# Where two sets of casts stand in ScalarE's order, and where three small tiles live, in a gated linear-attention kernel

## The chip, the cores and the metric

One core of one Trainium2 chip runs the whole kernel. The metric is device time in microseconds (us) for one launch; the time of a version is the median of its runs. TensorE (PE) does the matmuls, VectorE (DVE) and ScalarE (ACT) read and write its results in PSUM, GpSimd (POOL) works on SBUF alone, SyncE (SP) issues most of the transfers. Each engine runs its own instructions strictly in the order written for it: an instruction that waits holds up everything behind it on its engine.

## The reference, cut to what matters

```
xn  = layernorm(x)                                   # x: 2048 x 576
q, k, v = split(xn @ wqkv)                           # 32 heads of 18
phi(t) = concat(softmax(t @ w_phi), softmax(-(t @ w_phi)))   # per head
o   = phi(q) (phi(k)^T v) / (phi(q) . sum(phi(k)) + 1e-6)    # linear attention
s   = o @ wo
g   = silu((silu(xn @ w_gate) * (xn @ w_up)) @ w_down)       # F = 4608
out = x + s * g
```

All is fp32. A product of two fp32 operands is done as three matmuls of rounded parts: `split(hi, lo, src)` (line 57) makes `hi` by a cast on ACT (line 58) and `lo = src - hi` by a subtraction on DVE (line 59).

## The kernel before, in words

The kernel has four stages on the one core: layernorm, transposes and weight folding; the k/v stage, which sums phi(k)^T v over 16 row tiles; the q stage (lines 522 to 642); and the feed-forward part (FFN, from line 644), which takes two thirds of the time and is fed by gate/up weights (`gate_up_weights`, line 669), cast on ACT and subtracted on DVE, four pieces for each slice of the hidden layer.

**The q stage.** A query tile t has 128 rows; pairs of tiles go through a loop of nine steps (line 624). `q_tile` (line 558) makes the logits in the PSUM tile `p2` (line 563, 28 matmuls), then `softmax_parts` (line 273) takes the maximum and the minimum per head (line 278), subtracts them into the two halves of `e` (line 279) and takes two exponentials on ACT (line 282). After them VectorE has a chain of one tile: the sum `sm` (line 285), `ez = e * zb` (line 567), its sum `y` (line 569), five short ones, and the scaling of `e` (line 577). There is one `p2`: the next tile's logits wait until line 279 has read the present ones twice. `numer` (line 580) transposes `e` and multiplies with the k/v sums; `project` (line 598) multiplies with wo, which has been split into `WOH` and `WOL` by `split_wo` (line 533), copies each half row tile from PSUM into `so` on ACT (line 619) and stores it to `s_dram` from ACT's queue. In the last step of the loop (`last`) four such outputs remain: two share one `p2`, the third takes `p`, the fourth takes `p2` again. wo comes in by five loads into three staging tiles that borrow places of tiles used later: `oh`, `ol` and `ez` (lines 528 to 531).

**Filler for TensorE.** `early_tile` (line 113) does five of the 36 hidden slices early, so that TensorE has work while a chain runs on the others. Its products fill a bank `pe` with 14 matmuls; there are two banks. The first bank of a pair comes free by a silu on ACT (line 119), the second by a product on DVE (line 122). Its weights are split by lines 62 to 64. `tails` (line 541) prepares a part of the FFN's weights through the tile `tl` (two places): load, four subtractions on POOL, a cast on ACT (line 550), a subtraction on DVE (line 551), stores from POOL's queue.

**What sets the order.** The order on each engine is fixed when the program is built. The builder takes the order of the code as priority (`high_priority` lifts a block) and puts next the instruction of highest priority that it expects to be ready; what it expects to be ready early can thus come ahead of code written before it. `tc.issue_after(x)` queues the block's instructions **on x's engine** behind x; the block's instructions on other engines are not bound by it. A tile of a pool takes one of its tag's `bufs` places and holds it until its last reader has finished.

`read` collects the subtractions of line 279, which run on DVE; `split_wo` puts its instructions behind the last of the second query tile's.

Of the kernel before, what the change touches and what calls it, by code (L numbers as in the profile page):

```python
# [9 lines left out]
F32 = mybir.dt.float32  # L10
F32R = mybir.dt.float32r
AF = mybir.ActivationFunctionType
# [4 lines left out]
S, D, H, DH, F = 2048, 576, 32, 18, 4608  # L17
P = 128
# [5 lines left out]
HALF = D // 2  # L24
# [13 lines left out]
def heads(ap):  # L38
    return ap.rearrange("p (h d) -> p h d", d=DH)
# [7 lines left out]
def gated_hedgehog_kernel(ctx: ExitStack, tc, x, w_qk, w_v, w_phi, wo, w_gu, w_tail, w_down, ident_in, mask_in, out):  # L47
# [5 lines left out]
    nc = tc.nc  # L53
# [3 lines left out]
    def split(hi, lo, src):  # L57
        nc.scalar.copy(hi, src)  # L58
        nc.vector.tensor_sub(lo, src, hi)  # L59
# [53 lines left out]
    def early_tile(f, i, parts, js=(0, 1), banks=None):  # L113
        for j in js:
            pg, pu = banks or [eps.tile([P, BT], F32, name="pe") for _ in range(2)]
            xw(pg, i, j, slice(0, BT), *parts[0], False)
            h = epool.tile([P, BT], F32, name="h")
            with tc.high_priority():
                nc.scalar.activation(h, pg, AF.Silu)  # L119
            last = xw(pu, i, j, slice(0, BT), *parts[1], False)  # L120
            with tc.high_priority():
                nc.vector.tensor_mul(h, pu, h)
            nc.sync.dma_start(h_dram[i, f, :, j * BT:(j + 1) * BT], h)
        return last

    with ExitStack() as att:
        const = att.enter_context(tc.tile_pool(name="const", bufs=1))
        ident = const.tile([P, P], F32, name="ident")
# [7 lines left out]
        with ExitStack() as wst:  # L136
# [129 lines left out]
            kk = kst.enter_context(tc.tile_pool(name="kk", bufs=2, side="right", reuse_waits="tile"))  # L266
# [6 lines left out]
            def softmax_parts(ps, e):  # L273
                m = kk_pool.tile([P, 2, H], F32, name="m", bufs=1)
                p4 = ps[:, :, 0:HALF].rearrange("p a (h d) -> p a h d", d=DH)
                for s, op in enumerate((ALU.max, ALU.min)):
                    m3 = m[:, s].rearrange("p (a h) -> p a h", a=2)
                    nc.vector.tensor_reduce(m3, p4, axis=AX.X, op=op)
                    read.append(nc.vector.tensor_sub(e[:, s * D:(s + 1) * D].rearrange("p (a h d) -> p a h d", a=2, d=DH),
                                                     p4, m3.unsqueeze(3).to_broadcast([P, 2, H // 2, DH])))  # L280
                for s in range(2):
                    nc.scalar.activation(e[:, s * D:(s + 1) * D], e[:, s * D:(s + 1) * D], AF.Exp,
                                         scale=1.0 if s == 0 else -1.0)
                sm = kk_pool.tile([P, 2 * H], F32, name="sm")
                nc.vector.reduce_sum(sm, heads(e), axis=AX.X)
                return sm

            kk_pool, read = kk, []

            def kv_step(n, phi, v):  # L290
                for i in range(2 * NG):
# [108 lines left out]
            def k_tile(t):  # L400
                i0, j0, cols = block(t)
                pk = kps.tile([P, 2, 512], F32, name="p2")
                for i in range(2):
                    w = slice(i * HALF, (i + 1) * HALF)
                    xw(pk[:, i, 0:HALF], i0, j0, cols, KVWH[:, :, :, w], KVWL[:, :, :, w], True)
                phi = kk.tile([P, 2 * D], F32, name="phi", bufs=2)
                sm = softmax_parts(pk, phi)
                nc.vector.reciprocal(sm, sm)
                nc.vector.tensor_mul(heads(phi), heads(phi), spread(sm, 2 * H))
                return phi  # L410
# [111 lines left out]
        with ExitStack() as qst:  # L522
            qw = qst.enter_context(tc.tile_pool(name="qw", bufs=1, reuse_waits="tile"))
            qk = qst.enter_context(tc.tile_pool(name="qk", bufs=2, reuse_waits="tile"))
# [1 line left out]
            WOH = qw.tile([GW, NG, D], F32R, name="WOH")  # L526
            WOL = qw.tile([GW, NG, D], F32R, name="WOL")
            wrs = [qk.tile([P, 2, D], F32, name="oh", bufs=1), qk.tile([P, 2, D], F32, name="ol", bufs=1),
                   qk.tile([P, 2, D], F32, name="ez", bufs=1)]
            for g, (o, w) in enumerate(GROUPS):  # L530
                nc.sync.dma_start(wrs[g // 2][0:w, g % 2], wo[o:o + w, :])

            def split_wo():
                with tc.issue_after(read[-1].ins):
                    for n, wr in enumerate(wrs):
                        g, w = slice(2 * n, min(2 * n + 2, NG)), GROUPS[2 * n][1]
                        split(WOH[0:w, g], WOL[0:w, g], wr[0:w, 0:min(2, NG - 2 * n)])

            kk_pool = qk
# [58 lines left out]
            def project(b, oh, ol, last):  # L598
                for j in range(QS // P):
                    pair = qps.tile([P, 2, 512], F32, name="p2") if last and j == 0 else None  # L600
                    jc = slice(j * P, (j + 1) * P)
                    r0 = b * QS + j * P
                    for i in range(2):
                        n = slice(i * HALF, (i + 1) * HALF)
                        if pair:
                            ps = pair[:, i]
                        elif last and i:
                            ps = qps.tile([P, 2, 512], F32, name="p2")[:, 0]
                        else:
                            ps = qps.tile([P, 512], F32, name="p")  # L610
                        k = 0
                        for g, (o, w) in enumerate(GROUPS):
                            for a, bw in ((oh, WOH), (oh, WOL), (ol, WOH)):
                                nc.tensor.matmul(ps[:, 0:HALF], a[0:w, g, jc], bw[0:w, g, n], start=k == 0,  # L614
                                                 stop=k == 3 * NG - 1)
                                k += 1
                        so = qk.tile([P, HALF], F32, name="so", bufs=2)
                        with tc.high_priority() if last else ExitStack():
                            nc.scalar.copy(so, ps[:, 0:HALF])
                        nc.scalar.dma_start(s_dram[r0:r0 + P, n], so)  # L620

            order = list(range(S // QS // 2, S // QS)) + list(range(S // QS // 2))
# [1 line left out]
            for n in range(S // QS + 1):  # L624
                new = []
                if n > 0:
                    om = numer(es)
                if n < S // QS:
                    new += [q_tile(order[n] * (QS // P) + j) for j in range(QS // P)]
                if n == 0:  # L630
                    split_wo()
                if n > 0:
                    project(order[n - 1], *om, n == S // QS)
                es = new
# [34 lines left out]
    def gate_up_weights(i, f):  # L669

        parts, wt = {}, fw.tile([96, 7, P], F32R, name="wt", bufs=2)
        n, q = divmod(f - EARLY, 4)
        if i == 0:
            ld = fw.tile([P, 2, D], F32, name="ld", bufs=2).rearrange("p a b -> p (a b)")
            ld = ld[:, 0:8 * P].rearrange("p (m c n) -> p m c n", m=4, c=2)
            nc.sync.dma_start(ld, w_gu[f, :, :, 0:2])
            ts = fw.tile([P, D], F32, name="ts")[:, 0:4 * P].rearrange("p (m c n) -> p m c n", m=2, c=2)

        def ready(m, src):
            k = 1 if m == 6 else 2  # L680
            w = fw.tile([P, k, 4, P], F32R, name=f"w{k}", bufs=2 if k == 1 else 4)
            if i:
                nc.sync.dma_start(w.bitcast(F32), w_dram[f - EARLY, :, m:m + k])
            else:
                split(w[:, :, 0:2], w[:, :, 2:4], src)
                if f < NF - 1:
                    nc.sync.dma_start(w_dram[f - EARLY, :, m:m + k], w.bitcast(F32))
            for c in range(k):
                parts[m + c] = w[:, c]

        ready(0, None if i else ld[:, 0:2])
        nc.sync.dma_start(wt.bitcast(F32), t_dram[n, q].rearrange("b r m n -> (b r) m n"))
        if i == 0:
            nc.gpsimd.tensor_sub(ts[:, 0], ld[:, 2], ld[:, 0])
            nc.gpsimd.tensor_sub(ts[:, 1], ld[:, 3], ts[:, 0])
            nc.gpsimd.tensor_sub(ld[:, 2], ld[:, 3], ld[:, 2])
            nc.gpsimd.tensor_sub(ld[:, 1], ld[:, 1], ts[:, 1])  # L697
        ready(4, None if i else ts)
        ready(2, None if i else ld[:, 2:4])
        ready(6, None if i else ld[:, 1:2])  # L700
        return parts, wt
# [319 lines left out]
    todo = [(i, f) for i, n, f in units if f >= EARLY and (i == 0 or f < NF - 1)]  # L1021
# [5 lines left out]
        nc.sync.dma_start(t, w_down[f * P:(f + 1) * P, :])  # L1027
    xo = operands(0)
    early_tile(EARLY - 1, 0, parts)
    ready = [gate_up_weights(*todo.pop(0))]  # L1030
    est.close()
    fq = ctx.enter_context(tc.tile_pool(name="fq", bufs=1, reuse_waits="tile"))
    fps = ctx.enter_context(tc.tile_pool(name="fps", bufs=1, space=PSUM, reuse_waits="tile"))
# [72 lines left out]
```

## Time and profile before

| | |
|---|---|
| median of 3 runs | 1637.58 us (1636.6 to 1639.58) |
| the profiled execution | 1638.38 us, of which its span 1636.6 us |
| busy in the span | PE 1604.0, DVE 1168.5, ACT 721.9, POOL 653.3 us |
| q stage, from its first logits | 229.7 us on |
| last output copy of the q stage | 483.92 us |
| first FFN product with gate/up weights | 512.6 us |

A row of the timeline gives the start, the length, the engine and line, the operation with the tile written and the tiles read, the count of merged instructions, and in brackets how long the engine stood idle before it and what ended that wait. A row of the windows gives, for one stretch of the span, its length and then the busy time of each engine in it with the count of instructions. Times are us from the span's start.

### The profile page before, as it was taken

How to read it: one execution, taken by the hardware profiler on the slowest of the kernel's cores; microseconds unless marked ns; L12 is line 12 of the kernel's file. 1: busy time of each engine (PE TensorE's matmuls, PEld its weight loads, DVE VectorE, ACT ScalarE, POOL GpSimd, SP SyncE). 2: the span in 40 equal slices, each digit the busy share in tenths (PEclk: the TensorE clock that was granted, in tenths of full speed). 3: DMA queues.
4: the chain of work that ended last, by engine and by line, in shares of the span. 5: the costliest groups of instructions: out<-in, count | busy, mean ns of one | idle time of the engine just before them, and what ended most of it. 6: DMA issues, size and time to landing. Idle time of an engine off the chain costs nothing.

```text
span 1636.6 us, 25198 instructions
## 1 busy us (share of the span) xinstructions
PE 1604.0 (98%) x9385; PEld 1429.7 (87%) x9385; DVE 1168.5 (71%) x1721; ACT 721.9 (44%) x1391; POOL 653.3 (40%) x699
## 2 busy tenths in 40 slices
PE   6999998999999999999999999999999999999998
PEld 5899997999978888888888888888888888888887
DVE  7677768899952678778777778825666766666578
ACT  5533345444432554544444544455433433333334
POOL 3485661333212455455545355313233324133132
PEclk9999999999999999999999999999999999999999
DMA  9622243334248545555554554684454655555444
GB/s 286 206 80 78 85 134 117 117 103 126 67 144 306 184 165 175 179 178 168 177 180 165 175 192 152 224 296 150 136 162 135 199 184 170 172 179 185 140 115 174
DMA packets 121741, 268.46 MB, mean 164 GB/s; under 512 B 12787, under 2 KB 53363, under 8 KB 119827
## 3 DMA queue, kind: packets, MB, share of 16 engines
q1 hardware_dynamic: 106652, 246.49, 45.9%
q0 software_dynamic: 3072, 11.02, 2.4%
q10 hardware_dynamic: 11894, 9.35, 1.8%
q8 instruction: 74, 1.21, 0.3%
q14 instruction: 49, 0.39, 0.1%
HBM read 167.19 MB, written 99.61 MB: 163 GB/s over the span
## 4 chain that ended last, share of the span: by engine, by line
PE 90%; DMA 4%; DVE 3%; POOL 1%; issue 1%; ACT 1%; SPq 0%; ACTq 0%; POOLq 0%; DVEq 0%
PE px L707 24%; PE pd L832 24%; PE pw L707 12%; PE py L707 6%; PE p L92 6%; PE pe L92 5%; PE p L614 4%; PE po L594 2%; PE kvp L294 2%; PE vx L382 1%; PE pt L588 1%; DMA xn<-in_A_x 1%; PE vw L382 1%; DMA s_dram<-so 1%; DMA sraw<-in_A_w_v 1%
## 5 line engine op out<-in xcount | busy, mean ns | idle before, releaser
L832 PEld LDWEIGHTS pd<-dw,hh 128*128 128x128 f32 x3048 | 432.4, 188 | 26.4 <-DVE dw L59 1.7
L832 PE MATMUL pd<-dw,hh 128*128 128x288 f32 x3048 | 448.5, 297 | 4.3 <-DVE dw L59 1.5
L707 PE MATMUL px<-X,w 128*128 128x512 f32 x1488 | 384.3, 393 | 0.0
L707 PEld LDWEIGHTS px<-X,w 128*128 128x128 f32 x1488 | 270.6, 188 | 51.8 <-ACT s L736 2.0
L707 PE MATMUL pw<-X,w 128*128 128x512 f32 x732 | 188.7, 393 | 0.0
L707 PEld LDWEIGHTS pw<-X,w 128*128 128x128 f32 x732 | 137.0, 188 | 30.5
L741 DVE TENSOR_TENSOR s<-pw,s 128x512 f32<-128x512 f32 x124 | 85.1, 688 | 100.0 <-ACT s L736 89.2
L957 DVE TENSOR_TENSOR acc<-pd,acc 128x576 f32<-128x576 f32 x128 | 96.2, 752 | 83.8 <-PE pd L832 83.6
L736 ACT COPY s<-px 128x512 f32<-128x512 f32 x124 | 72.6, 585 | 157.2 <-PE px L707 157.2
L92 PE MATMUL pe<-X,wh 128*128 128x512 f32 (+1 forms) x380 | 121.8, 401 | 5.8 <-ACT h L119 2.9
L59 DVE TENSOR_TENSOR hh<-ha,hh 128x512 fp32r<-128x512 f32 x140 | 111.5, 823 | 20.7 <-ACT hh L58 19.1
L58 ACT CAST hh<-ha 128x512 fp32r<-128x512 f32 x140 | 82.7, 619 | 92.4 <-PE pd L832 73.5
L929 POOL TENSOR_TENSOR hb<-hb 128x512 f32<-128x512 f32 x34 | 47.0, 1381 | 168.6 <-DVE hb L753 161.4
L59 DVE TENSOR_TENSOR w<-ld,w 128x512 fp32r<-128x512 f32 (+1 forms) x93 | 77.2, 832 | 35.7 <-ACT w L58 34.5
L707 PE MATMUL px<-X,wt 96*128 96x512 f32 x248 | 97.9, 395 | 0.0
L707 PE MATMUL py<-X,w 128*128 128x512 f32 x372 | 96.5, 394 | 0.0
L916 POOL TENSOR_TENSOR h<-ha,hb 128x512 f32<-128x512 f32 x34 | 44.3, 1302 | 126.8 <-DVE ha L757 88.6
L942 POOL TENSOR_TENSOR ha<-ha 128x512 f32<-128x512 f32 x34 | 52.6, 1564 | 103.5 <-DVE hh L59 103.5
L58 ACT CAST w<-ld 128x512 fp32r<-128x512 f32 (+1 forms) x93 | 51.0, 549 | 89.6 <-POOL ld L697 56.8
L92 PEld LDWEIGHTS pe<-X,wh 128*128 128x128 f32 (+1 forms) x380 | 70.0, 189 | 21.7 <-ACT h L119 3.4
L761 ACT COPY py<-px 128x512 f32<-128x512 f32 x62 | 35.5, 572 | 102.7 <-PE px L707 80.8
L707 PEld LDWEIGHTS py<-X,w 128*128 128x128 f32 x372 | 66.7, 188 | 11.2
(262 smaller groups left out, 3199.0 us busy)
## 6 DMA issues: line engine op xcount, KB each, us to landing
w_dram<-w SPq DMA_DIRECT2D x90, 512.0 KB, 2.9
w<-w_dram SPq DMA_DIRECT2D x90, 512.0 KB, 4.5
wt<-t_dram SPq DMA_DIRECT2D x61, 336.0 KB, 3.7
ld<-in_B_w_gu SPq DMA_DIRECT2D x31, 512.0 KB, 4.5
X<-sum_dram SPq DMA_DIRECT2D x8, 1280.0 KB, 11.1
rt<-in_B_w_down SPq DMA_DIRECT2D x33, 288.0 KB, 3.1
rb<-in_B_w_down SPq DMA_DIRECT2D x33, 288.0 KB, 4.7
w_dram<-w SPq DMA_DIRECT2D x30, 256.0 KB, 2.1
```

Of the source, the lines that this page charges most:

```text
L58: nc.scalar.copy(hi, src)
L59: nc.vector.tensor_sub(lo, src, hi)
L92: last = nc.tensor.matmul(ps, l, r, start=n == 0, stop=n == len(pairs) - 1)
L614: nc.tensor.matmul(ps[:, 0:HALF], a[0:w, g, jc], bw[0:w, g, n], start=k == 0, stop=k == 3 * NG - 1)
L707: nc.tensor.matmul(ps, l, r, start=first and n == 0, stop=last and n == len(mm) - 1, skip_group_check=True)
L736: nc.scalar.copy(t, ps)
L741: nc.vector.tensor_add(t, ps, t)
L832: nc.tensor.matmul(ps, l, r, start=first and n == 0 and m == 0, stop=n == len(hs) - 1 and m == 2, skip_group_check=True)
L916: sub(s, g["h"][0][0], g["h"][0][1])
L929: nc.gpsimd.tensor_add(a21, a21, g["h"][1][1])
L942: sub(a12, a12, g["h"][0][0])
L957: nc.vector.tensor_add(a2, pd[:, :, 0:HALF], a2)
```

## The change

Two edits, each with a change of place for the tiles it concerns.

- `split_wo`'s block is bound to `exps[-1]`, the second exponential of the second query tile on ACT, in place of `read[-1]` on DVE. The casts into `WOH` are now behind that exponential; the subtractions into `WOL` are bound only by needing the casts.
- The third staging tile of wo takes one of the four places of `e`, no longer the one place of `ez`.
- All output copies are collected in `outs`; the first call of `gate_up_weights` is queued on ACT behind the last of them.
- In the last step of the q loop, the second half row tile of each output goes through a place of `tl`, no longer of `so`.

```diff
+    outs = []
...
-                    nc.scalar.activation(e[:, s * D:(s + 1) * D], e[:, s * D:(s + 1) * D], AF.Exp,
-                                         scale=1.0 if s == 0 else -1.0)
+                    last = nc.scalar.activation(e[:, s * D:(s + 1) * D], e[:, s * D:(s + 1) * D], AF.Exp,
+                                                scale=1.0 if s == 0 else -1.0)
+                exps.append(last)
...
-            kk_pool, read = kk, []
+            kk_pool, read, exps = kk, [], []
...
             wrs = [qk.tile([P, 2, D], F32, name="oh", bufs=1), qk.tile([P, 2, D], F32, name="ol", bufs=1),
-                   qk.tile([P, 2, D], F32, name="ez", bufs=1)]
+                   qk.tile([P, 2 * D], F32, name="e", bufs=4).rearrange("p (a n) -> p a n", a=2)]
...
             def split_wo():
-                with tc.issue_after(read[-1].ins):
+                with tc.issue_after(exps[-1].ins):
...
-                        so = qk.tile([P, HALF], F32, name="so", bufs=2)
+                        if last and i:
+                            so = qk.tile([P, 7, P], F32, name="tl", bufs=2).rearrange("p a n -> p (a n)")[:, 0:HALF]
+                        else:
+                            so = qk.tile([P, HALF], F32, name="so", bufs=2)
                         with tc.high_priority() if last else ExitStack():
-                            nc.scalar.copy(so, ps[:, 0:HALF])
+                            outs.append(nc.scalar.copy(so, ps[:, 0:HALF]))
...
-    ready = [gate_up_weights(*todo.pop(0))]
+    with tc.issue_after(outs[-1].ins):
+        ready = [gate_up_weights(*todo.pop(0))]
```

## Prediction

> **What bounds the kernel now.** The page comes first: how much of the span is TensorE's own work.
>
> ```profile
> span 1636.6 us, 25198 instructions
> PE 1604.0 (98%) x9385; PEld 1429.7 (87%) x9385; DVE 1168.5 (71%) x1721; ACT 721.9 (44%) x1391; POOL 653.3 (40%) x699
> ```
>
> TensorE is idle for 1636.6 - 1604.0 = 32.6 us. The change removes no matmul, so it can win only idle time of TensorE, in the places that it reaches. The windows show how much lies there: length of the stretch, then PE, PEld, DVE, ACT and POOL busy.
>
> ```profile
> 240.00:280.00 40.00, 35.84 (x205) 30.68 (x205) 34.21 (x51) 22.00 (x28) 7.59 (x16) 1.00 0.46 146
> 280.00:460.00 180.00, 179.99 (x1235) 165.89 (x1234) 164.07 (x259) 80.68 (x144) 54.48 (x112) 1.00 0.33 100
> 470.00:490.00 20.00, 17.93 (x94) 14.25 (x93) 7.94 (x11) 7.04 (x15) 7.32 (x8) 1.00 0.72 238
> ```
>
> At the start of the q stage TensorE is idle for 40.00 - 35.84 = 4.16 us, at its end for 20.00 - 17.93 = 2.07 us, and between them for 0.01 us in 180. So 6.2 us, 0.38% of the time, is all that there is to win. TensorE's timeline shows it as six waits:
>
> ```profile
> 255.40 0.50 PE L92 MATMUL pe<-X,wh 128*128 128x512 f32 x1 [1.19 <-ACT h L119]
> 260.49 0.50 PE L92 MATMUL pe<-X,wh 128*128 128x512 f32 x1 [1.55 <-DVE h L122]
> 270.36 0.37 PE L92 MATMUL p<-QH,X 128*128 128x288 f32 x1 [1.42 <-DVE e L279]
> ...
> 477.94 0.40 PE L614 MATMUL p<-WOH,oh 126*128 126x288 f32 x1 [1.17 <-ACT so L619]
> 485.39 0.50 PE L92 MATMUL pe<-X,wh 128*128 128x512 f32 x1 [0.28 <-ACT h L119]
> 489.57 0.47 PE L92 MATMUL pe<-X,wh 128*128 128x512 f32 x1 [0.63 <-ACT h L119]
> ```
>
> I call them A, B, C and D, E1, E2. A and B wait for a filler bank that ACT or DVE frees late, C for the logits' only tile, which DVE reads late, D for an output copy. Why these engines are late is in their own timelines, ACT first:
>
> ```profile
> 239.61 1.26 ACT L282 ACTIVATE e<-e 128x576 f32<-128x576 f32 x2
> 244.86 1.16 ACT L58 CAST WOH<-oh 126x1152 fp32r<-126x1152 f32 x1 [3.99 <-DMA oh<-in_A_wo]
> 248.05 1.16 ACT L58 CAST WOH<-ol 126x1152 fp32r<-126x1152 f32 x1 [2.04 <-DMA ol<-in_A_wo]
> 249.12 0.66 ACT L58 CAST WOH<-ez 72x576 fp32r<-72x576 f32 x1
> 251.19 0.94 ACT L550 CAST th<-tl 128x896 fp32r<-128x896 f32 x1 [1.41 <-POOL tl L549]
> 252.04 0.68 ACT L282 ACTIVATE e<-e 128x576 f32<-128x576 f32 x1
> ...
> 254.75 0.60 ACT L119 ACTIVATE h<-pe 128x512 f32<-128x512 f32 x1
> ...
> 256.66 0.69 ACT L282 ACTIVATE e<-e 128x576 f32<-128x576 f32 x1
> ```
>
> After the first tile's exponentials ACT stands still for wo's transfers (3.99 and 2.04 us) and then for the tail's (1.41). The second tile's exponentials and the silu that ends A come behind all that. VectorE:
>
> ```profile
> 243.00 1.35 DVE L285 TENSOR_REDUCE sm<-e 128x64 f32<-128x1152 f32 x1
> ...
> 246.51 0.76 DVE L279 TENSOR_TENSOR e<-p,m 128x576 f32<-128x576 f32 x1
> 247.19 1.35 DVE L59 TENSOR_TENSOR WOL<-oh,WOH 126x1152 fp32r<-126x1152 f32 x1
> 253.47 0.69 DVE L63 TENSOR_TENSOR wl<-raw,wh 128x512 fp32r<-128x512 f32 x1 [4.94 <-ACT wh L62]
> ...
> 255.90 0.75 DVE L59 TENSOR_TENSOR WOL<-ez,WOH 72x576 fp32r<-72x576 f32 x1
> ...
> 257.24 1.34 DVE L567 TENSOR_TENSOR ez<-e,zb 128x1152 f32<-128x1152 f32 x1
> ...
> 259.76 0.68 DVE L122 TENSOR_TENSOR h<-pe,h 128x512 f32<-128x512 f32 x1
> ...
> 269.46 0.75 DVE L279 TENSOR_TENSOR e<-p,m 128x576 f32<-128x576 f32 x1
> ```
>
> It stands idle for 4.94 us up to 253.47 and then runs without a break. The first tile's `ez` product at 257.24 could have run at 244.35, when `sm` was done, but its place held the last wo rows until 255.90 + 0.75 = 256.65. So `ez` and what follows it come when they delay the product that ends B (259.76) and the subtraction that ends C (269.46).
>
> **The change part by part.**
>
> *The place of the last wo rows.* No instruction is added. `ez` of the first tile can start at 244.35 and fill the hole. What fits: `ez` (1.34, the row at 257.24), the sum `y` of the same size (I take 1.34), and the short ones, in all up to the 4.94 us that are idle now, less the 1.35 of `WOL<-oh`, which leaves its place at 247.19 for a later one. VectorE is thus ahead by up to 4.94 at 253 and has then 1.35 more to do: a net lead of 3.59 us. At most, that is: if only `ez` and `y` go forward, it is 2.68 - 1.35 = 1.33. B is 1.55 and C 1.42. The lead needn't pay both: TensorE, once B is gone, arrives at C 1.55 us earlier, so both together need 2.97. I take the larger end, 3.59, since the whole chain of the first tile is free to run in that hole and no other work of VectorE's is ready there. **B and C go: 2.97 us.** The price is that the second tile's subtractions of line 279 may come behind `ez` and `y`, later by up to 2.68 us than 246.51; the logits of the third tile wait for that, and filler covers it as long as a bank is free. The fourth place of `e` is first wanted by the fourth tile, whose logits start at 270.36, long after the rows have been split; I cost that at nothing.
>
> *The binding of the casts.* It takes 1.16 + 1.16 + 0.66 = 2.98 us of casts out of ACT's wait for wo and puts them behind the exponential that now ends at 256.66 + 0.69 = 257.35. That gains little at A: `th<-tl` at 251.19 comes later in the code than the second tile's exponentials, yet stands ahead of them in ACT's order, so the builder expects it to be ready sooner. It will still stand there, and still wait until 251.19. The silu that ends A comes behind it. From below A could shrink to nothing, if the silu comes ahead of that cast; from above it could grow by the 2.98 us of the casts, if these come ahead of the silu. I take **A as it is, 1.19**, since the row at 251.19 doesn't move. Behind the casts are queued the silus and exponentials after 257.35; ACT is busy for only 22.00 of the 40 us, and that hides 2.98. WOH and WOL are first read much later:
>
> ```profile
> 276.76 0.38 PE L614 MATMUL p<-WOH,oh 126*128 126x288 f32 x1
> ```
>
> The casts would end near 257.35 + 2.98 = 260.3, the subtractions (1.35, one like it, 0.75: 3.45 us) soon after, with some 12 us to spare.
>
> [...] VectorE would now run products of two SBUF tiles beside POOL's four subtractions for the tail, which end at 251.16 and release `th<-tl`. What that costs POOL can be read elsewhere in this trace:
>
> ```profile
> 477.12 0.72 POOL L694 TENSOR_TENSOR ts<-ld 128x256 f32<-128x256 f32 x1 [46.30 <-DMA ld<-in_B_w_gu]
> 483.69 1.07 POOL L694 TENSOR_TENSOR ts<-ld 128x256 f32<-128x256 f32 x1 [3.33 <-DVE w L59]
> 483.48 2.70 DVE L59 TENSOR_TENSOR w<-ld,w 128x512 fp32r<-128x512 f32 x3
> ```
>
> The same subtraction took 0.72 us alone and 1.07, half as much again, while VectorE subtracted from SBUF. The four subtractions before 251.16 lie in 1.95 us (1.41 of them as ACT's wait), so half as much again is about 1 us more, and `th`, the silu and A would all be later by that. It is a rival below. [...]
>
> *The end of the q stage.* ACT's order there:
>
> ```profile
> 473.36 0.40 ACT L619 COPY so<-p 128x288 f32<-128x288 f32 x1 [1.02 <-PE p L614]
> ...
> 476.97 0.62 ACT L58 CAST w<-ld 128x512 fp32r<-128x512 f32 x1 [3.22 <-DMA ld<-in_B_w_gu]
> 477.50 0.39 ACT L619 COPY so<-p 128x288 f32<-128x288 f32 x1
> 481.18 0.40 ACT L619 COPY so<-p 128x288 f32<-128x288 f32 x1 [3.29 <-DMA s_dram<-so]
> ```
>
> The second copy stands behind a weight cast that waits 3.22 us for its load; the fourth output's matmuls wait for that copy, and this is D. With the cast behind all four copies, the second runs at about 473.8, and **D goes: 1.17 us**. The third copy's 3.29 us wait for a place goes too, with four places for four outputs; `tl` is free, since POOL's last store from it is issued well before:
>
> ```profile
> 428.83 2.00 POOL L554 DMA_DIRECT2D t_dram<-tl  x4 [3.34 <-DVE tl L551]
> ```
>
> The added wait: the first weight's casts wait for the fourth copy, where the first started at 476.97. The fourth output's last matmul:
>
> ```profile
> 479.92 0.30 PE L614 MATMUL p<-WOH,ol 72*128 72x288 f32 x1
> ```
>
> Without D it ends at 480.22 - 1.17 = 479.05, so the casts start about 2.5 us later than now. Behind them on ACT are the casts of the second weight and the filler's silus. The weights are first wanted at 512.8:
>
> ```profile
> L707 PE MATMUL px<-X,w x1488: 387/393/501, 512.8 to 1612.5; 128*128 128x512 f32 x186
> ```
>
> More than 30 us of filler cover that. E1 and E2 (0.91 together) are silus that come late among these casts. They may go or stay, or double; I leave them.
>
> *The sum:* B 1.55 + C 1.42 + D 1.17 = 4.14 us. The profiled execution took 1638.38 (span 1636.6 and 1.78 around it), so 1634.24; it lies 0.80 above the median of the three runs, so **1633.4** as a median.
>
> **The rivals.** All are given as medians.
>
> *Nothing is left of the six waits.* The silu of A comes ahead of `th`, or the order gives TensorE the third tile's logits to do meanwhile, and E1 and E2 go with the lighter load. For: ACT has 10 us between 240.87 and 251.19 in which it now has nothing to do. Against: the silu must be ready by then in the builder's expectation, and it stood behind `th`. 6.23 us less: 1631.3.
>
> *The first edit does not do what it says.* The wait for wo was never the last one: ACT stands at `th` until 251.19 with or without wo's casts, the second tile's exponentials come when they came, the builder puts VectorE's chain where it was, and B and C remain. For: the 1.41 us wait at 251.19 is the one that ends last. Against: the `ez` place. Only D goes: 1636.4.
>
> *Slower: the casts get in front of a bank's release.* They used to lie inside a wait; now they are work in the busiest place. If the order puts the three between the second tile's exponential and the silu that ends A, A grows by 2.98. If VectorE's order does not use the hole, `WOL<-oh` leaves it, and VectorE, which has no idle time from 253.47 on, is later by 1.35 at B and again at C, since each of these waits is for its own instruction. It decides at the order: from the point at which that silu stands behind the casts. For: silu and exponential already alternate there. Against: the silu has `high_priority`, the casts have none. At most 2.98 + 1.35 + 1.35 - 1.17 = 4.5 us more: 1642.1.
>
> *POOL's share.* The forecast with `th` later by about 1 us: 1634.4.
>
> **How the numbers follow.** A measurement of this kernel tells about 0.2%, 3.3 us, from no change. Chances: forecast 0.45 (own range 1632.0 to 1635.0), no waits left 0.15, only D 0.23, slower 0.13, POOL's share 0.04. Faster by over 0.2% means under 1634.3: all of "no waits left" and nearly all of the forecast, 0.57. Slower by over 0.2% means above 1640.9; of the slower rival, whose price is an upper one, I count most, 0.12. The rest, 0.31, is within 0.2%. The range is 1631.0 to 1639.0: it holds all but the slower rival and a tail on either side.
>
> **What would show it.** In the profile of the changed kernel: the window 240 to 280 with TensorE busy about 38.8 us, and only the wait for `h L119` near 255 left; VectorE's `ez` of the first tile before 250 and no 4.94 us idle; ACT's first instruction after about 241 is not a cast of `WOH`, and `th` still starts near 251.2; four output copies in a row, none waiting for `s_dram`, and no TensorE wait for `so`. The prediction is wrong if `th` moves, if TensorE shows a new wait for `p2` or `pe` of over 2 us, or if stretches that the change does not name (280 to 460, or after 490) lose or win more than 1 us.

## The result, and the profile after

The changed kernel takes **1710.25 us** (median of 6 runs, 1707.43 to 1712.79) where the kernel before, beside it, takes 1638.77: a ratio of 1.0439 (95% interval 1.0427 to 1.0450), 71.5 us slower. The forecast was 1633.4. Both edits do what the diff says, and something that neither names costs ten times what they could win.

The page of the changed kernel first: span, busy times, and TensorE, POOL and the granted clock in 40 slices of 42.8 us.

```profile
span 1710.9 us, 25186 instructions
...
PE 1616.3 (94%) x9385; PEld 1438.1 (84%) x9385; DVE 1168.8 (68%) x1721; ACT 722.0 (42%) x1391; POOL 653.5 (38%) x699
...
PE   6999999999993299999999999999999999999998
...
POOL 3476640000045754644653544522342243132222
PEclk9999999999996599999999999999999999999999
```

TensorE's idle time is 1710.9 - 1616.3 = 94.6 us against 32.6, +62.0. Its busy time has grown as well, by 12.3 us, with the same 9385 matmuls; together that is the 74.3 us by which the span grew. Most of both lies in slices 13 and 14 of TensorE's row, and there the clock row falls to 6 and 5 tenths. POOL's row shows something else, and earlier: five slices of nothing, from the seventh on. The windows (length, then PE, PEld, DVE, ACT and POOL busy, clock, DMA share, GB/s) put numbers on that:

```profile
280.00:460.00 180.00, 179.90 (x1213) 164.41 (x1213) 151.85 (x245) 74.91 (x136) 0.00 (x0) 1.00 0.09 32
470.00:490.00 20.00, 20.00 (x124) 17.66 (x125) 8.07 (x14) 8.89 (x19) 3.62 (x5) 1.00 0.40 126
490.00:538.00 48.00, 37.77 (x147) 29.36 (x146) 8.73 (x12) 8.20 (x14) 22.67 (x43) 0.91 0.88 311
538.00:546.00 8.00, 0.00 (x0) 0.00 (x0) 1.09 (x1) 0.06 (x1) 7.36 (x16) 0.50 0.61 172
546.00:900.00 354.00, 305.81 (x1644) 267.94 (x1645) 245.13 (x342) 161.07 (x318) 199.19 (x234) 0.92 0.53 176
```

From 280 to 460 POOL did 54.48 us of work before; now it does none, and TensorE is still full. From 470 to 490 TensorE has no idle time any more: D, E1 and E2 are gone, as meant (a new wait of 0.79 us, for the filler's product, stands at 497). After 490 it stands for 10.2 + 8.0 + 48.2 us. What went missing is seen by tile: `tl`, in which the tails are prepared, first before and then after (instructions, shortest/median/longest in ns, first and last start in us).

```profile
L544 SPq DMA_DIRECT2D tl<-in_B_w_tail x8: 327/328/429, 243.0 to 401.6; - x8
L546 POOL TENSOR_TENSOR tl<-tl x8: 452/462/672, 249.2 to 410.4; 128x128 f32<-128x128 f32 x8
```

```profile
L546 SPq DMA_DIRECT2D tl<-in_B_w_tail x8: 328/332/533, 486.3 to 574.7; - x8
L548 POOL TENSOR_TENSOR tl<-tl x8: 465/466/910, 489.6 to 582.0; 128x128 f32<-128x128 f32 x8
...
L552 ACT CAST th<-tl x8: 935/937/942, 493.8 to 584.0; 128x896 fp32r<-128x896 f32 x8
...
L624 ACT COPY tl<-p x2: 400/400/401, 484.0 to 486.8; 128x288 f32<-128x288 f32 x2
```

All eight tails, loaded from 243 to 402 before, are now loaded from 486.3 on: the first of them takes the place that the first output copy (484.0) and its store leave. What this costs TensorE is in its timeline, all its waits from 500 to 640:

```profile
519.15 0.80 PE L712 MATMUL px<-X,wt 96*128 96x512 f32 x1 [3.38 <-DMA wt<-t_dram]
585.49 2.93 PE L712 MATMUL px<-X,w 128*128 128x512 f32 x6 [53.56 <-ACT s L741]
589.62 2.93 PE L712 MATMUL px<-X,w 128*128 128x512 f32 x6 [0.77 <-ACT s L741]
600.10 4.85 PE L712 MATMUL px<-X,w 128*128 128x512 f32 x12 [5.05 <-DVE hb L758]
609.37 1.65 PE L712 MATMUL px<-X,w 128*128 128x512 f32 x6 [0.46 <-ACT s L741]
616.97 1.32 PE L837 MATMUL pd<-dw,hh 128*128 128x288 f32 x8 [1.58 <-DVE dw L59]
625.17 1.66 PE L712 MATMUL px<-X,w 128*128 128x512 f32 x6 [0.74 <-ACT s L741]
```

First the FFN waits for a tail itself (`wt` is read from `t_dram`); then, for 53.56 us, for a plain copy from PSUM on ACT. That copy has no wait of its own. It stands behind casts that do, in ACT's timeline:

```profile
537.12 0.94 ACT L552 CAST th<-tl 128x896 fp32r<-128x896 f32 x1 [9.22 <-POOL tl L551]
546.35 0.94 ACT L552 CAST th<-tl 128x896 fp32r<-128x896 f32 x1 [8.29 <-POOL tl L551]
...
584.02 0.94 ACT L552 CAST th<-tl 128x896 fp32r<-128x896 f32 x1 [8.76 <-DMA t_dram<-tl]
584.86 0.58 ACT L741 COPY s<-px 128x512 f32<-128x512 f32 x1
```

Six tails in a row, 9.2 to 9.7 us apart. POOL sets this pace:

```profile
538.36 4.02 POOL L556 DMA_DIRECT2D t_dram<-th  x8 [0.59 <-ACT th L552]
542.36 2.00 POOL L556 DMA_DIRECT2D t_dram<-tl  x4
544.38 0.47 POOL L548 TENSOR_TENSOR tl<-tl 128x128 f32<-128x128 f32 x1
```

Twelve stores of 0.5 us each to issue, then four subtractions in the 1.97 us from 544.38 to the next cast at 546.35, that cast, 537.12 to 538.36 with its way to POOL: 6.02 + 1.97 + 1.24 = 9.23. This is the reading to take along from the view: the line that TensorE waits for (L741) is blameless, and one looks at what stands in front of it on its engine.

### The profile page after: what moved, and what is told of

The parts are those of the page before. It is cut to its first block, busy times and chain, and to the rows that moved or that the text cites. A ratio compares the mean times of both kernels' runs of the same rounds, so it can differ in the third digit from the quotient of the medians.

```text
span 1710.9 us, 25186 instructions
## 1 busy us (share of the span) xinstructions
PE 1616.3 (94%) x9385; PEld 1438.1 (84%) x9385; DVE 1168.8 (68%) x1721; ACT 722.0 (42%) x1391; POOL 653.5 (38%) x699
## 4 chain that ended last, share of the span: by engine, by line
PE 86%; DMA 4%; POOL 4%; DVE 3%; issue 1%; ACT 1%; ACTq 0%; SPq 0%; POOLq 0%; DVEq 0%
PE px L712 23%; PE pd L837 23%; PE pw L712 11%; PE p L92 6%; PE py L712 6%; PE pe L92 4%; PE p L616 4%; POOL t_dram L556 2%; PE po L596 2%; PE kvp L296 2%; PE vx L384 1%; DMA t_dram<-tl 1%; PE pt L590 1%; DMA xn<-in_A_x 1%; PE vw L384 1%
## 5 line engine op out<-in xcount | busy, mean ns | idle before, releaser
L712 PE MATMUL px<-X,w 128*128 128x512 f32 x1488 | 390.2, 398 | 60.6 <-ACT s L741 55.5
L699 POOL TENSOR_TENSOR ts<-ld 128x256 f32<-128x256 f32 x31 | 26.8, 865 | 329.3 <-DMA ld<-in_B_w_gu 254.7
L741 ACT COPY s<-px 128x512 f32<-128x512 f32 x124 | 72.7, 586 | 156.6 <-PE px L712 156.6
L59 DVE TENSOR_TENSOR w<-ld,w 128x512 fp32r<-128x512 f32 (+1 forms) x93 | 77.3, 832 | 36.2 <-ACT w L58 35.1
```

The source lines that it names most:

```text
L712: nc.tensor.matmul(ps, l, r, start=first and n == 0, stop=last and n == len(mm) - 1, skip_group_check=True)
L741: nc.scalar.copy(t, ps)
```

## The experiments

TensorE's idle time and its busy time are told apart, since both differ; each line is the profiled execution, with the clock granted from 240 to 280. The medians and ratios (95% intervals) are of all runs, against the kernel before on the same chip. Of the idle time 15.7 to 18.2 us lie ahead of 120 us, in stages that no edit touches, so a difference of one or two us in that column doesn't speak of an edit by itself; the single waits do.

| version | median us, ratio | span | PE busy | PE idle | clock 240 to 280 |
|---|---|---|---|---|---|
| before | | 1636.6 | 1604.0 | 32.6 | 1.00 |
| changed | 1710.25, 1.0439 | 1710.9 | 1616.3 | 94.6 | 0.96 |
| e2_tl_only | 1705.11, 1.0409 (1.0395 to 1.0423) | 1703.4 | 1615.2 | 88.2 | 0.91 |
| e8_no_lift | 1713.0, one run | 1711.1 | 1616.5 | 94.6 | 0.91 |
| e1_out_ph | 1643.48, 1.0033 (1.0020 to 1.0046) | 1643.9 | 1606.5 | 37.4 | 0.91 |
| e3_tails_first | 1643.38, 1.0031 (1.0020 to 1.0042) | 1639.5 | 1604.4 | 35.1 | 1.00 |
| e4_wo_only | 1641.32, 1.0014 (1.0003 to 1.0024) | 1639.9 | 1606.8 | 33.1 | 0.91 |
| e5_bind_only | 1640.10, 1.0020 (1.0009 to 1.0031) | 1639.8 | 1607.3 | 32.5 | 0.96 |
| e6_place_only | 1643.19, 1.0042 (1.0029 to 1.0056) | 1643.8 | 1608.5 | 35.3 | 0.91 |
| e9_both_bound | 1644.30, 1.0045 (1.0032 to 1.0058) | 1642.9 | 1607.1 | 35.8 | 0.91 |
| e11_late_e | 1644.19, 1.0034 (1.0021 to 1.0048) | 1642.5 | 1607.2 | 35.3 | 0.96 |
| e7_out_only | 1637.15, 0.9998 (0.9989 to 1.0007) | 1637.5 | 1605.5 | 32.0 | 1.00 |
| e12_ph_only | 1638.53, 1.0002 (0.9993 to 1.0011) | 1637.1 | 1603.6 | 33.5 | 1.00 |
| e10_bind_out | 1636.93, 0.9996 (0.9988 to 1.0005) | 1636.2 | 1603.4 | 32.8 | 1.00 |

**The theory** after the result: places of a tile are promised in the order of the code. The last `project` stands in the code ahead of the loop that writes the tails, so its two outputs take the two places of `tl` first, and every tail is put behind them. Rivals: the first edit upsets the tails (it moves the casts that `th` stood among); or the `high_priority` on the output copies pulls the tile forward.

### Where the tails went

*The one suspect line alone.* The kernel before, with only this:

```diff
-                        so = qk.tile([P, HALF], F32, name="so", bufs=2)
+                        if last and i:
+                            so = qk.tile([P, 7, P], F32, name="tl", bufs=2).rearrange("p a n -> p (a n)")[:, 0:HALF]
+                        else:
+                            so = qk.tile([P, HALF], F32, name="so", bufs=2)
```

> The kernel before with only the place of the last outputs' second halves changed, so to tl; no binding is added. Theory (places): this line alone brings the loss, 1700 to 1715, with POOL idle from 280 to 460 and a wait of some 50 us near 535. Rival (binding): the loss needs the weight casts bound behind the outputs; then this one is within 1630 to 1645.

Measured 1705.11, +66.7 us of the 71.5. By tile, the tails moved as in the changed kernel, and TensorE waits for the same copy:

```profile
L544 SPq DMA_DIRECT2D tl<-in_B_w_tail x8: 327/332/595, 484.7 to 566.3; - x8
```

```profile
576.98 2.93 PE L710 MATMUL px<-X,w 128*128 128x512 f32 x6 [45.59 <-ACT s L739]
```

*The whole change, the halves through another tile's place* (`ph`, whose last regular use is ahead of these outputs in the code):

```diff
-                            so = qk.tile([P, 7, P], F32, name="tl", bufs=2).rearrange("p a n -> p (a n)")[:, 0:HALF]
+                            so = qk.tile([P, 2 * QS], F32, name="ph", bufs=2)[:, 0:HALF]
```

> The changed kernel with one thing different: the second half of the last outputs goes through a place of ph, no longer of tl. Theory (places): the eight tails came after the q stage only because the outputs, written earlier in the code, hold the two places of tl; without that the tails are back between 250 and 430 us, POOL is busy there again, the 53.6 us wait of TensorE is gone, and what is left is the two small wins seen in the changed kernel's windows (TensorE idle 2.4 in place of 4.2 us in 240 to 280, 0 in place of 2.1 in 470 to 490): about 1635, 1632 to 1637. Rival (wo): the late casts of wo or the bound weight casts push the tails and the first weights back by themselves: 1700 or more as before, POOL still idle from 280 to 460.

Measured 1643.48: 66.8 us below the changed kernel by the medians. The tails' loads are back at 243.0 to 398.6. But the time is not the expected 1632 to 1637: about 5 us above the kernel before are left, and the next part looks for them.

*The whole change with `tl` kept, but the tails written first.*

```diff
+                if n == S // QS:
+                    for m in range(TAILS):
+                        with tc.issue_after(last_e[3 * m // 2 + 2].ins):
+                            tails(m)
                 if n > 0:
                     project(order[n - 1], *om, n == S // QS)
                 es = new
-            for n in range(TAILS):
-                with tc.issue_after(last_e[3 * n // 2 + 2].ins):
-                    tails(n)
```

> The changed kernel, tl for the outputs kept, but the loop that writes the tails stands in the code ahead of the last project. Theory (places are promised in the order of the code): the tails get the places first, the outputs after them: no loss, 1632 to 1638. Rival (the copies' high_priority takes the places, or tl is too small for both): still 1700 or more.

Measured 1643.38, again above the expected 1632 to 1638. The outputs still use `tl`; only the order of two blocks in the code has changed, and that is worth 66.9 us:

```profile
L546 SPq DMA_DIRECT2D tl<-in_B_w_tail x8: 327/328/430, 242.3 to 394.0; - x8
...
L624 ACT COPY tl<-p x2: 399/400/400, 485.1 to 487.8; 128x288 f32<-128x288 f32 x2
```

*The whole change, the copies not lifted.*

```diff
-                        with tc.high_priority() if last else ExitStack():
+                        with ExitStack():
```

> The whole change, but the last outputs' copies without high_priority, so that the code asks for the two places of tl in the same order and only the order on ACT can move. Theory (places of tl are given in the order of the code, the outputs standing ahead of the tails): as the change, about 1710 us, POOL without work from 241 to about 482. Rival (the lift of the copies pulls their places ahead of the tails): the tails return to 250 to 410, POOL works there, and the time is about 1640.

One run: 1713.0, and the tails as in the changed kernel:

```profile
L546 SPq DMA_DIRECT2D tl<-in_B_w_tail x8: 328/333/517, 486.0 to 574.9; - x8
```

So the cause of the large loss is settled: not the first edit, not the lift, but the order in which the code asks for the places of `tl`.

### The first edit

*Alone, both halves of it* (the kernel before with the binding to the exponentials and the rows in `e`):

> The kernel before with the first edit alone: casts of wo behind the second query tile's exponentials, last wo rows in a place of e. Theory (places): this part is a small win, TensorE idle in 240 to 280 down from 4.2 to about 2.4 us, so 1635 to 1638. Rival (wo): it costs, by casts and subtractions in the busy stretch from 255 on: 1641 or more, with new waits of TensorE for pe or p.

*Its binding alone* (`issue_after(exps[-1].ins)`, the last wo rows left in `ez`):

> The kernel before with the casts of wo bound behind the second query tile's exponentials, and nothing else; the last wo rows stay in ez. Theory (place): the new waits of TensorE at the start of the q stage (0.7 and 1.65 us near 242) come from the place in e, not from the binding: here VectorE's first subtractions into e stay near 234.5, right behind the maximum. ez of the first tile is late as before, so B and C stay in some form: 1637 to 1641. Rival (binding): the binding moves them, and they show here too.

*Its place alone* (rows in `e`, the binding left at `read[-1]`):

> The kernel before with the last wo rows in a place of e, and nothing else. Theory (place): the first query tile now gets another place of e, the builder holds it ready later, and the filler's product (line 122) goes ahead of the first subtraction into e: VectorE idle for some 5.8 us near 236 to 242, TensorE waiting 0.7 and 1.65 us near 242: about 1641, 1639 to 1644. Rival (binding): the first subtraction stays near 234.5, and the time is at or under that of before.

Measured 1641.32, 1640.10 and 1643.19: each slower than before, the place by 6.0 us. For the whole edit the rival came true and not the small win; the binding and the place came out within their ranges. The table splits what the profiled executions lose: the whole edit 2.8 us of busy time and 0.5 of idle, the binding 3.3 of busy time and none of idle, the place 4.5 and 2.7. So more than half is TensorE working longer at the same matmuls; that part is taken up in the last section, the waits here.

In TensorE's timeline of the version with everything but the lost tails (e3_tails_first), the first stretch of the q stage has these waits:

```profile
241.73 0.47 PE L92 MATMUL pe<-X,wh 128*128 128x512 f32 x1 [0.70 <-DVE h L122]
243.85 0.37 PE L92 MATMUL p<-QH,X 128*128 128x288 f32 x1 [1.65 <-DVE e L280]
254.43 0.50 PE L92 MATMUL pe<-X,wh 128*128 128x512 f32 x1 [0.52 <-ACT h L119]
256.25 0.37 PE L92 MATMUL p<-QH,X 128*128 128x288 f32 x1 [1.33 <-DVE e L280]
```

B and C are gone, as forecast, and A has shrunk to 0.52. But 0.70 + 1.65 at 242 and 1.33 at 256 are new: 4.20 us in all, where A, B and C were 4.16. The two at 242 are in every version with the rows in the first place of `e` and unbound filler (the changed kernel, e1, e3, e4, e6, e8) and in none with the rows in `ez`. VectorE's timeline of the changed kernel shows what makes them:

```profile
235.50 0.76 DVE L279 TENSOR_REDUCE m<-p 128x32 f32<-128x576 f32 x1 [0.68 <-PE p L92]
242.12 0.69 DVE L122 TENSOR_TENSOR h<-pe,h 128x512 f32<-128x512 f32 x1 [5.86 <-PE pe L92]
242.73 0.75 DVE L280 TENSOR_TENSOR e<-p,m 128x576 f32<-128x576 f32 x1
```

The first tile's maximum is ready at 236.3 and its subtraction waits for nothing, yet it stands behind the filler's product, which waits 5.86 us for its bank. Two runs ask whether the place is the reason. The first binds the filler behind the subtraction:

```diff
-                early_tile(f, i, parts, (1,) if f == 1 else (0, 1))
+                with tc.issue_after(read[2 * NT + 1].ins) if f == 1 else ExitStack():
+                    early_tile(f, i, parts, (1,) if f == 1 else (0, 1))
```

> The changed kernel with the outputs through ph, and the filler's first product bound behind the first query tile's second subtraction into e. Theory (place): this one order undoes the new waits near 242 (0.7 and 1.65 us) and lets VectorE's hole be filled as forecast: TensorE idle in 240 to 280 at most 2.5 us, and 1 to 3 us less than with the outputs through ph alone (1643.5): 1640 to 1642.5. If the waits at the FFN's start are still there (5 us), it is not under before. Rival: the waits near 242 have another cause and stay.

The second asks for the rows' place in `e` only after the first two tiles have theirs, in `split_wo`, and loads them there; both stand on e1_out_ph. The two lines that matter:

```diff
+                wrs.append(qk.tile([P, 2 * D], F32, name="e", bufs=4).rearrange("p (a n) -> p a n", a=2))
+                wo_rows(list(enumerate(GROUPS))[4:])
```

> The whole change with the outputs through ph, and the last wo rows in a place of e that the code asks for only after the first two tiles have theirs; so the first tile keeps its first place and ez is free for it. Theory (the price of the place in e is only that the first tile gets another place): the two waits at 242 (0.70 and 1.65) are gone, B and C stay away, and the time is 2.4 us below the version with only the outputs moved to ph, ratio about 1.001 or lower. Rival (what is taken from these waits comes back at A, because ACT's cast of the tail waits for its load and the silu stands behind it): no wait at 242 but 3 to 4 us at A, ratio 1.003 again.

Measured 1644.30 and 1644.19, neither within its theory's range. In both the waits at 242 are gone; by e11_late_e, the place handed to the first tile was indeed the reason. And in both A has grown, from 2.35 in e1_out_ph to 4.06 and 3.34. The waits of this stretch together are 4.24 and 4.21 us against 5.72 there; of these 1.5 us the medians show nothing, and their intervals of some 2 us on either side could hide it. Of e11_late_e, TensorE and then ACT:

```profile
254.20 0.50 PE L92 MATMUL pe<-X,wh 128*128 128x512 f32 x1 [3.34 <-ACT h L119]
256.03 0.58 PE L92 MATMUL p<-QH,X 128*128 128x288 f32 x1 [0.87 <-DVE e L280]
```

```profile
250.57 0.94 ACT L556 CAST th<-tl 128x896 fp32r<-128x896 f32 x1 [9.34 <-POOL tl L555]
251.41 0.83 ACT L62 CAST wh<-raw 128x768 fp32r<-128x768 f32 x1
252.26 1.28 ACT L119 ACT_TABLE_LOAD   x1
253.55 0.60 ACT L119 ACTIVATE h<-pe 128x512 f32<-128x512 f32 x1
```

ACT stands for 9.34 us at the tail's cast, and the silu that frees the bank comes behind it. TensorE has run out of banks at 254.20 - 3.34 = 250.86, before that cast is done at 251.51; 3.34 + 0.87 = 4.21 is the old 4.16 once more. Here the rival that was on record for this run came true: most of what is taken away ahead of that cast returns at it.

The cast is not the only late one there, though. In the changed kernel no tail is cast in this stretch, and ACT stands nearly as long for the load of the filler's weights, which the same silu is behind:

```profile
252.35 0.83 ACT L62 CAST wh<-raw 128x768 fp32r<-128x768 f32 x1 [6.69 <-DMA raw<-in_B_w_gu]
```

In e3_tails_first, e4_wo_only and e1_out_ph ACT waited for this load once more behind the tail's cast, for 0.24, 0.66 and 0.78 us. So two transfers bound the stretch, and it is not shown that moving the tail's cast alone would free the bank.

### The second edit

*Alone, through `ph`* (the kernel before, with the weight casts bound behind the last output copy):

> The kernel before with the second edit alone, but through a place of ph, no longer tl: the first weights' casts behind the last output copy. Theory (as forecast): D, E1 and E2 go, 2.1 us, 1636 to 1637. Rival (passed on): the weight casts, later by some us, put the first FFN slices' order wrong, with waits of TensorE for s (line 736) of 4 to 5 us between 525 and 555: 1640 or more.

*The places alone, without that binding:*

> Before, with the outputs' second halves in places of ph and nothing else: neither of the two bindings, the wo rows in ez. Two of the four copies have a place of their own, but one weight cast, which waits for its load, still stands ahead of the third copy on ACT. Theory (D is the copy behind the weight cast): a wait of TensorE for that copy stays, between 0.5 and 1.2 us, the waits A, B, C are as before, the FFN's start waits as before (2.6), and the time is within 0.1% of before. Rival (D is the want of a place for the third copy): D is gone without the binding, and the stretch 460 to 500 is as full as in the version with both, 39.99 of 40.

With the binding, TensorE has no wait left at the end of the q stage:

```profile
460.00:500.00 40.00, 39.99 (x217) 33.30 (x216) 14.41 (x23) 12.02 (x26) 9.10 (x11) 1.00 0.61 208
```

But the time is the same, 1637.15 against 1637.18; the interval rules out a win of 2.07 us, though not one of 1.17. Without the binding, D stays, and is now for `ph`, in TensorE's timeline and in ACT's:

```profile
477.71 0.40 PE L614 MATMUL p<-WOH,oh 126*128 126x288 f32 x1 [1.27 <-ACT ph L622]
```

```profile
476.74 0.62 ACT L58 CAST w<-ld 128x512 fp32r<-128x512 f32 x1 [3.01 <-DMA ld<-in_B_w_gu]
477.27 0.39 ACT L622 COPY ph<-p 128x288 f32<-128x288 f32 x1
```

So D was the copy behind the weight cast, as the prediction had it, and not the want of a place: a place for each output wins nothing by itself, and `tl` was not needed for it. Where did the 2.07 us go? In the profiled execution of e7_out_only, the slowest of its eleven runs, A was 2.22 instead of 1.19, TensorE's busy time was 1.5 us longer, and the FFN's start waits longer. Before, and then e7_out_only:

```profile
540.20 0.53 PE L832 MATMUL pd<-dw,hh 128*128 128x288 f32 x2 [1.10 <-DVE hh L59]
542.23 1.33 PE L832 MATMUL pd<-dw,hh 128*128 128x288 f32 x8 [1.50 <-DVE dw L59]
```

```profile
521.95 1.66 PE L711 MATMUL px<-X,w 128*128 128x512 f32 x6 [1.00 <-ACT s L740]
539.33 0.53 PE L836 MATMUL pd<-dw,hh 128*128 128x288 f32 x2 [0.70 <-DVE hh L59]
541.37 1.95 PE L836 MATMUL pd<-dw,hh 128*128 128x288 f32 x8 [1.50 <-DVE dw L59]
```

That is 2.60 and 3.20. These waits are 2.19 in e12_ph_only and 5.67 in e3_tails_first. In the latter, which is the whole change without the lost tails, the FFN's start thus takes 3.07 us more than before, and that is more than the 2.07 won at the end of the q stage. Whether the order of the casts, of the loads or of POOL's subtractions decides there wasn't tried and stays open.

*What might win: the binding of the casts, and the second edit through `ph`, the wo rows in `ez`:*

> Before, with the casts of wo bound behind the second tile's exponentials, the last wo rows kept in ez, the outputs' second halves through places of ph, the weight casts bound behind the last output copy. Theory (the binding alone takes C, 1.42, and the outputs' part takes D and E, 2.07; what is given back is at the FFN's start, 0.4 to 0.6, and at A by the load times, up to 1): 1634 to 1637 us against the same chip's before at 1637, that is a ratio of 0.998 to 1.0. Rival (every gain ahead of the FFN is given back at its start, whatever was won, because the FFN's first tiles are bound to loads and casts of their own): ratio 1.0 with over 3 us of TensorE waits after 525.

Measured 1636.93 against 1637.32, ratio 0.9996 with 1 inside its interval. A, B and C are 1.01, 1.71 and 1.11 (3.83 of 4.16), D and E are gone, and the FFN's start takes 3.74 instead of 2.60. The time lies in the theory's range, but the ratio and the waits at the FFN's start are also the rival's, so this run doesn't decide between them. The binding costs 2.9 us by itself (e5_bind_only) and nothing together with the second edit; the granted clock differs (0.997 in the mean of those runs, 0.998 here), why is open. No version here beats the kernel before by more than its interval.

## Why the prediction was wrong

**The step that failed** is in "The end of the q stage": "`tl` is free, since POOL's last store from it is issued well before [428.83]". That is a time of the kernel before. It holds only as long as the tails come when they came, and the edit took the very place that let them come. A borrowed place is not free because its users finish early; it is free if the borrower asks for it after them. The text of the code says which: `project` for the last step stands above the loop of the tails. Price: 66.7 us alone. The warning that closed the prediction (stretches after 490 that lose over 1 us) is what happened, with no rival and no chance for it. Without this step the forecast would still have been too good: e1_out_ph and e3_tails_first, which keep the rest of the change, took 1643.4 to 1643.5 and not 1633.4. The other steps say where that went.

**"No instruction is added", "B and C go: 2.97 us", and the place in `e` "at nothing".** B and C did go, and the first tile's `ez` moved, to 248.20 in the changed kernel (forecast from 244.35 on). What failed is the price: alone, the place costs 6.0 us (e6_place_only). I asked only when the fourth tile wants its place, not which place the first tile gets once another asker stands ahead of it. New waits of 0.70, 1.65 and 1.33 (e3_tails_first) replaced what was won.

**"A as it is, 1.19", `th` unmoved.** Right in kind: `th` starts at 250.45 in e3_tails_first, 250.67 in e10_bind_out and 252.33 in e1_out_ph (251.19 before), and A is 0.52, 1.01 and 2.35 there; it goes with `th`, not with wo's casts. What the step missed is the use of this fact: that cast, with the filler's load beside it, comes last in the stretch, so most of a gain ahead of it is not kept.

**D.** Mechanism right (e12_ph_only), and E1 and E2, which I left alone, went too: 2.07 instead of 1.17. **"More than 30 us of filler cover that"** held for the weights' arrival, but the waits of the FFN's start grew by 0.6 (e7_out_only), 1.1 (e10_bind_out) and 3.1 us (e3_tails_first).

**A term that the sum doesn't have** is TensorE's clock: it counts idle time alone, and a wait can also be followed by longer matmuls, 0.80 us for one after 2.35 in e1_out_ph, where the same one after 1.19 took 0.50 in the kernel before (last section).

**The rivals.** "Slower, the casts in front of a bank's release" had the right sign and neither the mechanism nor the size: the three casts stood behind the silu that ends A, at 256.85 to 259.62 against 253.78 in e3_tails_first. "Only D" is nearest to e7_out_only, which won 0.03 us of the 1.17; the interval there can't tell the two apart. No run shows the microsecond of "POOL's share": in e3_tails_first the four subtractions from 248.46 on take 0.46 us each, as before, but beside VectorE's two reductions (248.24 and 248.91), not beside the `ez` product, which is over by 248.32. What the changed kernel shows is elsewhere: of the first tail's four, the two that start at 489.56 and 491.31 took 0.91 and 0.90 us, and began while VectorE subtracted (488.92 to 491.90); the two after that took 0.46 each. (The row of 0.72 us that the prediction calls alone has VectorE's subtraction of 477.62 beside its last 0.22 us.)

## What to carry to other kernels

Before a tile borrows another's place, look in the code at who asks first, not in the profile at when the place was last used: with places promised in code order, the borrower that stands above the owner's loop sends the whole loop behind itself, on every engine it uses. When one wait is taken away, look for the instruction that comes last in that stretch whatever you do (here a cast that waits for a transfer); as long as it stands ahead of the release, most of the gain comes back there as another wait. When the busy time of TensorE grows with the same matmuls (here by 12.3 us), look at the granted clock behind each wait (0.50 here, from 538 to 546). And a small win at the end of one stage has to be followed into the start of the next.

## What the runs showed of the hardware

**A wait can cost twice.** After a long wait matmuls can take nearly twice as long: 0.80 us for one after 3.38 (519.15 above), where one after 1.19 took 0.50 (255.40 in the kernel before); 2.93 for six after 53.56, where six after 0.46 took 1.65 (609.37 above). The clock granted in the whole window from 538 to 546 is 0.50. The smaller versions show it too. From 240 to 280, of e4_wo_only and then of e3_tails_first:

```profile
240.00:280.00 40.00, 35.80 (x181) 30.84 (x180) 33.80 (x50) 18.86 (x24) 7.63 (x16) 0.91 0.48 146
```

```profile
240.00:280.00 40.00, 35.80 (x203) 30.68 (x202) 36.09 (x54) 19.89 (x27) 7.58 (x16) 1.00 0.47 147
```

The same waits to 0.01 us and the same 35.80 us busy, but at 0.91 fewer matmuls are done in them: by estimate 0.09 of 40 us, 3.6 us of work at a clock of 1.00, is pushed out. In the table the versions with 0.91 or 0.96 there have 1606.5 to 1608.5 us of busy time, those with 1.00 have 1603.4 to 1605.5 (changed kernel, e2_tl_only and e8_no_lift apart, which lose more later). e5_bind_only has no more idle time than before, 32.5 us, and is 3.2 us longer.

Finer windows say how much. In windows of 0.5 us, up to the last matmul, a clock below 1.00 comes in stretches at 0.50, each 3.41 us long or a whole multiple of it: one in the kernel before (from 18.5 on), none in e10_bind_out, three in e4_wo_only (from 243.5, 257 and 550.5 on), a double one at 256.5 in e1_out_ph, and one of 58.03, seventeen times 3.41, at the long wait of the changed kernel. A stretch of 3.41 us in which TensorE is busy throughout thus costs 1.7 us, an estimate (half of 3.41). In windows of 1 us, TensorE's busy time multiplied by the share of the clock that was not granted, and added up, is 1.7 us for the kernel before, 14.1 for the changed one, 5.1 for e4_wo_only, 4.9 for e5_bind_only and 6.7 for e6_place_only: 12.4, 3.4, 3.2 and 4.9 more than before, where the busy time is 12.3, 2.8, 3.3 and 4.5 us longer. So to within 0.6 us the longer busy time is the clock, and with it most of what the profiled executions with the first edit lose; this is worked out from rows, no run held the clock still.

How long a wait has to be for this is not shown. In e1_out_ph a wait of 2.35 us was followed by a matmul of 0.80 us (256.84), in e7_out_only one of 2.22 by one of 0.50 (256.52), and in e11_late_e one of 3.34 by one of 0.50; there only after the next, 0.87, did one of 0.58 come (256.03 above), where the same matmul of e3_tails_first took 0.37 (256.25). And the waits of 4.20 us gave 0.91 in the execution of e4_wo_only and 1.00 in that of e3_tails_first.
